# A two-layer decode kernel: one pool for all chunk places, half of wo ahead of time, V four chunks behind K, evenly paced chain pieces, fused end

## Chip, cores and metric

The kernel runs on one core of one Trainium2 chip. The time is device microseconds of one execution; most executions of one kernel agree within 0.3%. Times were taken on several chips, so kernels are compared by ratios: the mean time of one kernel's fast runs over the mean of the other's fast runs of the same rounds. This is not quite the ratio of the medians that are also quoted.

## The reference, cut to what matters

Eight rows (batch), one token each, run through attention, an MLP block, and the same attention and MLP a second time with the same caches and weights.

```python
x = x + A(layernorm(x), k_cache, v_cache, wq, wo)   # layer 1
x = x + B(layernorm(x), w1, w2, w3, w4)
x = x + A(layernorm(x), k_cache, v_cache, wq, wo)   # layer 2, same caches
x = x + B(layernorm(x), w1, w2, w3, w4)
# B=8, D=448, 16 query heads, 8 K/V heads, 4096 keys, head size 256, F=1792, bf16
```

With one token, both kernels leave out B's w1/w2 branch, whose shifted columns are all zero. K and V of a row are 32 chunks of 1 MB. Both layers need all of them, but layer 2 of a row can only begin when the row's layer 1 is through its *chain*: wo, norm, w3, GELU, w4, norm and the next query projection.

## The kernel before

Two K/V heads make a *pair*: four K chunks and four V chunks. Ten of a row's chunks are *kept* in SBUF from layer 1 until layer 2; everything else goes through a ring of five places. Loads leave in one fixed order through one queue, and each load has its place fixed in advance:

```python
        if key in kept:
            where[it] = NS + kept.index(key)      # one of ten bound places
            if ps == 0: loads.append(it)
        else:
            where[it] = r % NS                    # ring of NS = 5
            r += 1; loads.append(it)
...
    def emit_loads(most=None):
        while loads and not held[where[loads[0]]] and n != most:
            it = loads.pop(0)                     # strictly in order
```

A K chunk is transposed on VectorE, multiplied by q on TensorE (scores); exponentials run on ScalarE; a V chunk is multiplied by the probabilities (PV). The chain of a row is a generator. Its pieces are put between the chunks as fast as one or two a step:

```python
    hurry = (0, 1, Bn - 2, Bn - 1)
    def step(item=True):
        for kind in ("chain", "last"): ...
            for _ in range(2 if item and b in hurry and kind == "chain" else 1):
                if next(g, gens) is gens: ...
```

The end of the program is serial: the last row's wo, norm, w3, GELU, w4, and an output row in one partition (`...` is cut):

```python
    nc.vector.tensor_mul(var, mv[:, 0, :], mv[:, 0, :])
    nc.vector.tensor_sub(var, mv[:, 1, :], var)
    nc.vector.tensor_scalar_max(var, var, 0.0)
    nc.vector.tensor_scalar_add(ve[:, 0, :], var, EPS)
    nc.vector.reciprocal(ve[:, 1, :], ve[:, 0, :])   # second of two norms in a row
...
    for c in range(HC):                              # 14 matmuls of 448 columns
        nc.tensor.matmul(o_row[:], HT[:, c, :], w4_sb[:, c, :], ...)
```

The softmax here doesn't subtract the row's maximum and nothing guards it: scores larger than these inputs give would overflow.

## Time and profile before

| | before |
|---|---|
| time, median of 4 runs | 1195.3 us (1194.5 to 1197.7) |
| profiled span | 1196.4 us (of an execution of 1198.7 us, 3.4 above the median) |
| data moved | 465.91 MB |
| TensorE / VectorE busy | 55% / 47% |

From the page of the kernel before: the span, TensorE's busy tenths in 40 slices of 30 us, the granted TensorE clock, the DMA engines' busy tenths, the rate, and what the chain of waits that ended last is made of.

```profile
span 1196.4 us, 36650 instructions
...
PE   3133674357634774357634675357743674368765
...
PEclk9999997555655566555655557555665557555555
DMA  9999999999999999999999999999999999999792
GB/s 350 375 421 420 407 343 407 420 418 325 378 422 420 392 414 412 420 421 373 418 421 420 399 397 404 422 420 382 420 420 421 398 354 405 420 410 346 280 360 124
...
DMA 54%; PE 22%; DVE 17%; SPq 3%; issue 2%; POOL 1%; DVEq 0%; POOLq 0%; ACT 0%; ACTq 0%
```

The rate has a plateau at 420 to 422 GB/s and dips below it; loads are the largest part of the chain of waits. So the span can be read as a floor, 465.9 MB at 421 GB/s = 1107 us, plus lost DMA time. In the windows view (start and length of a stretch, busy time of PE, PE's weight loads, DVE, ACT and POOL with instruction counts, granted clock, DMA share, GB/s) the loss of a stretch is length × (1 − GB/s / 421).

```profile
48.00:140.00 92.00, 36.70 (x898) 26.78 (x902) 42.98 (x27) 7.01 (x14) 0.00 (x0) 1.00 1.01 420
140.00:190.00 50.00, 37.26 (x1034) 30.89 (x1030) 23.54 (x55) 5.04 (x10) 1.26 (x2) 0.95 0.93 359
...
264.00:316.00 52.00, 39.89 (x1041) 32.37 (x1039) 25.47 (x57) 7.01 (x14) 1.25 (x2) 0.54 0.91 340
...
944.00:1000.00 56.00, 39.59 (x1150) 32.10 (x1146) 27.45 (x53) 6.64 (x13) 1.25 (x2) 0.61 0.95 364
...
1070.00:1104.00 34.00, 27.07 (x698) 22.86 (x700) 16.66 (x54) 4.07 (x9) 1.25 (x2) 0.51 0.93 348
1104.00:1160.00 56.00, 39.14 (x1134) 35.68 (x1126) 26.96 (x49) 5.73 (x12) 2.59 (x1) 0.55 0.81 311
...
1177.20:1196.40 19.20, 10.37 (x152) 6.55 (x152) 4.78 (x29) 0.21 (x1) 0.70 (x1) 0.61 0.00 1
```

The first line is an undisturbed stretch. The next four are *chain stretches*: a row's chain runs between the chunks, chunks are freed late, and the queue waits. The 1104 line is the last row's stretch, the last line the tail without loads.

Short pieces of the timeline (start, length, engine, line, operation; in brackets the idle time before it and what ended it).

At the end of the program: the last PV, the sum onto x, the last matmuls, the cast of the output row.

```profile
1177.23 1.01 PE L587 MATMUL o_111<-ptw,slot_79 128*128 128x2 bf16 x32 [0.98 <-DMA slot_79<-in_A_v_cache_dram]
...
1180.13 0.16 DVE L709 TENSOR_TENSOR xT<-xT,o_112 128x4 f32<-128x4 f32 x1 [1.60 <-PE o_112 L309]
...
1189.76 3.93 PE L725 MATMUL o_row<-w_sb,HT_t 128*1 128x448 bf16 x14
...
1193.72 0.61 DVE L734 CAST slot_87<-o_row 1x448 bf16<-1x448 f32 x1 [5.78 <-PE o_row L725]
```

The last PV waits for the last load, and 18.2 us (1178.2 to 1196.4) follow it.

### The profile page before, as it was taken

What the parts mean: (1) busy time and instruction counts of PE and PEld (TensorE: products, weight loads), DVE (VectorE), ACT (ScalarE), POOL (GpSimd) and SP (SyncE); (2) the same over time, 40 slices, a digit from 0 to 9 for tenths busy, and PEclk for the clock granted to TensorE, in tenths of its full rate; (3) what the DMA queues carried; (4) which work ended last, traced back from release to release, by engine and by line L of the source; (5) the groups of instructions that cost most, each with busy time, mean ns of one, the idle gap of its engine ahead of it and who ended that gap; (6) DMA issues with size and microseconds to landing.
All of it is one profiled execution on the core that took longest, in us unless ns stands there. A gap on an engine that the chain in (4) does not pass through costs nothing.

```text
span 1196.4 us, 36650 instructions
## 1 busy us (share of the span) xinstructions
PE 660.9 (55%) x17225; PEld 521.2 (44%) x17225; DVE 565.3 (47%) x770; ACT 115.4 (10%) x233; POOL 15.6 (1%) x25
## 2 busy tenths in 40 slices
PE   3133674357634774357634675357743674368765
PEld 2122553245423563246522564235532553256654
DVE  5144454445444535456444554445354535444451
ACT  0000101001110111010101011101110111011100
POOL 0000000000000000000000000000000000000000
PEclk9999997555655566555655557555665557555555
DMA  9999999999999999999999999999999999999792
GB/s 350 375 421 420 407 343 407 420 418 325 378 422 420 392 414 412 420 421 373 418 421 420 399 397 404 422 420 382 420 420 421 398 354 405 420 410 346 280 360 124
DMA packets 69494, 465.91 MB, mean 389 GB/s; under 512 B 7120, under 2 KB 13152, under 8 KB 13664
## 3 DMA queue, kind: packets, MB, share of 16 engines
q1 hardware_dynamic: 69344, 463.58, 96.1%
q8 instruction: 134, 2.20, 0.7%
q14 instruction: 16, 0.13, 0.0%
HBM read 463.54 MB, written 0.01 MB: 387 GB/s over the span
## 4 chain that ended last, share of the span: by engine, by line
DMA 54%; PE 22%; DVE 17%; SPq 3%; issue 2%; POOL 1%; DVEq 0%; POOLq 0%; ACT 0%; ACTq 0%
DMA slot_78<-in_A_k_cache_dram 10%; DMA slot_80<-in_A_k_cache_dram 8%; DMA slot_81<-in_A_k_cache_dram 8%; DMA slot_87<-in_A_k_cache_dram 7%; DMA slot_79<-in_A_k_cache_dram 6%; DMA slot_82<-in_A_k_cache_dram 6%; DMA slot_83<-in_A_k_cache_dram 5%; PE y_ps L309 5%; PE sc_110 L532 4%; PE sc_109 L532 4%; DMA slot_92<-in_A_k_cache_dram 3%; DVE slot_78 L525 3%; DVE slot_81 L525 3%; DVE slot_80 L525 2%; DVE slot_79 L525 2%; DVE slot_82 L525 2%
## 5 line engine op out<-in xcount | busy, mean ns | idle before, releaser
L532 PEld LDWEIGHTS <-qbd 128*8 128x8 bf16 x8192 | 199.6, 112 | 496.7 <-issue 340.3
L573 PEld LDWEIGHTS <-ptw 128*8 128x8 bf16 x3840 | 115.8, 116 | 45.0 <-issue 16.3
L525 DVE STREAM_TRANSPOSE slot_78<-slot_78 128x2048 uint32<-128x2048 uint32 x34 | 78.5, 2310 | 87.6 <-DMA slot_78<-in_A_k_cache_dram 87.5
L525 DVE STREAM_TRANSPOSE slot_82<-slot_82 128x2048 uint32<-128x2048 uint32 x31 | 71.6, 2309 | 65.1 <-DMA slot_82<-in_A_k_cache_dram 64.9
L525 DVE STREAM_TRANSPOSE slot_79<-slot_79 128x2048 uint32<-128x2048 uint32 x32 | 73.9, 2308 | 59.4 <-DMA slot_79<-in_A_k_cache_dram 59.1
L525 DVE STREAM_TRANSPOSE slot_80<-slot_80 128x2048 uint32<-128x2048 uint32 x33 | 76.2, 2308 | 43.2 <-DMA slot_80<-in_A_k_cache_dram 42.9
L525 DVE STREAM_TRANSPOSE slot_81<-slot_81 128x2048 uint32<-128x2048 uint32 x30 | 69.2, 2308 | 44.7 <-DMA slot_81<-in_A_k_cache_dram 44.3
L541 ACT ACTIVATE p_n<-sc_110 128x512 bf16<-128x512 f32 x32 | 42.3, 1321 | 338.3 <-PE sc_110 L532 338.3
L541 ACT ACTIVATE p_n<-sc_109 128x512 bf16<-128x512 f32 x32 | 42.3, 1322 | 314.0 <-PE sc_109 L532 314.0
L309 PEld LDWEIGHTS <-wo_sb 128*128 128x128 bf16 (+1 forms) x1600 | 63.3, 125 | 16.4 <-issue 15.9
L309 PE MATMUL y_ps<-OT,wo_sb 128*128 128x1 bf16 (+1 forms) x1280 | 52.2, 176 | 6.6 <-DVE OT L424 5.7
L265 PEld LDWEIGHTS <-wq_sb 128*128 128x128 bf16 x1152 | 34.9, 105 | 27.3 <-issue 25.5
L532 PE MATMUL sc_110<-slot_78,qbd 128*8 128x128 bf16 x480 | 15.6, 304 | 48.0 <-DVE slot_78 L525 41.0
L561 ACT CAST ptw<-misc 128x128 bf16<-128x128 f32 x64 | 17.6, 275 | 252.8 <-PE misc L554 248.2
L532 PE MATMUL sc_109<-slot_78,qbd 128*8 128x128 bf16 x608 | 18.9, 296 | 36.4 <-DVE slot_78 L525 29.2
L265 PE MATMUL q_ps<-xb_126,wq_sb 128*128 128x1 bf16 x1024 | 32.0, 165 | 12.6 <-DVE xb_126 L253 10.2
L532 PE MATMUL sc_109<-slot_80,qbd 128*8 128x128 bf16 x576 | 18.1, 299 | 31.4 <-DVE slot_80 L525 26.8
L532 PE MATMUL sc_109<-slot_81,qbd 128*8 128x128 bf16 x512 | 16.0, 298 | 30.0 <-DVE slot_81 L525 25.2
L291 DVE TENSOR_SCALAR qbd<-misc,quad 128x64 bf16<-128x64 f32 x64 | 13.9, 278 | 39.5 <-PE misc L285 39.5
L532 PE MATMUL sc_110<-slot_82,qbd 128*8 128x128 bf16 x576 | 18.1, 299 | 26.0 <-DVE slot_82 L525 21.8
L532 PE MATMUL sc_109<-slot_79,qbd 128*8 128x128 bf16 x448 | 14.0, 297 | 31.6 <-DVE slot_79 L525 27.0
L532 PE MATMUL sc_110<-slot_79,qbd 128*8 128x128 bf16 x576 | 17.8, 296 | 24.6 <-DVE slot_79 L525 18.3
(193 smaller groups left out, 896.4 us busy)
## 6 DMA issues: line engine op xcount, KB each, us to landing
slot_81<-in_A_v_cache_dram SPq DMA_DIRECT2D x40, 1024.0 KB, 10.3
slot_79<-in_A_v_cache_dram SPq DMA_DIRECT2D x39, 1024.0 KB, 9.0
slot_82<-in_A_v_cache_dram SPq DMA_DIRECT2D x39, 1024.0 KB, 11.4
slot_78<-in_A_v_cache_dram SPq DMA_DIRECT2D x37, 1024.0 KB, 9.0
slot_80<-in_A_v_cache_dram SPq DMA_DIRECT2D x37, 1024.0 KB, 10.5
slot_78<-in_A_k_cache_dram SPq DMA_DIRECT2D x34, 1024.0 KB, 10.5
slot_80<-in_A_k_cache_dram SPq DMA_DIRECT2D x33, 1024.0 KB, 11.3
slot_79<-in_A_k_cache_dram SPq DMA_DIRECT2D x32, 1024.0 KB, 9.7
```

The costliest lines, as they stand in the source:

```text
L265: nc.tensor.matmul(q_ps[:, j * Hq + h, :], w, xbs(nb)[:, xi, :], start=(fc == 0), stop=(fc == 3),)
L291: nc.vector.tensor_scalar_mul(qbd[:, :, :, a, :], qs.rearrange("p e (f g u h) -> p (e f) u g h", f=2, u=2, h=2)[:, :, u], quad[:, a : a + 1],)
L309: nc.tensor.matmul(r, w[:, i, lo:hi], rhs(i), start=(first and fc == 0 and i == rows[0]), stop=(stop and i == rows[-1]), skip_group_check= ...
L525: nc.vector.transpose(w, w)
L532: nc.tensor.matmul(sc[32 * k : 32 * k + 8, 128 * x : 128 * x + 128], qbd[:, ep, gp].rearrange("p a h -> p (a h)"), kv[:, k, 2 * half + e2, ...
L541: nc.scalar.activation(p_sb[:].rearrange("p t i x -> p x t i"), sc[:].rearrange("p (x t i) -> p x t i", x=4, t=4), ACT.Exp, scale=scale_ex ...
L561: nc.scalar.copy(ptw[:, :, :, 6:8], pt_ps.rearrange("p t k (a h) -> p a (t k) h", a=4),)
L573: nc.tensor.matmul(o_ps[32 * q : 32 * q + 8, 256 * (g // 4) : 256 * (g // 4) + 256], ptw[:, a, 4 * (y % 4) + y // 4, w : w + 8], v[:, y * ...
```

## The change

Its intent: let any freed place take the next load; take work out of the chain's tight stretch and spread the rest evenly; shorten the serial end. The core of the diff, with cuts:

```diff
-            where[it] = r % NS
+    places = list(range(NC))                     # NC = 15, one pool
...
-        while loads and not held[where[loads[0]]] and n != most:
+        while loads and places and n != most:
+            p = where[it] = places.pop(0)
...
-        if j >= 5:                               # V five chunks behind K
+        if j >= LAG:                             # LAG = 4
...
+    def first_half(b, st):                       # heads 0-7 through wo, early
+        yield from half(st["o"], st["z"], 0, OT[:, :, :, 0])
+        yield from add_half(y_ps, OT, 0, 1, True, 2)
...
+            if e["n"] < e["of"] * (idx - e["at"] + 1) / max(e["until"] - e["at"], 1):
+                e["n"] += 1                      # as many pieces as the items passed
...
+            nc.vector.scalar_tensor_tensor(var, mv[:, 0], mv[:, 0], mv[:, 1],
+                ALU.mult, ALU.subtract, reverse1=True)
+        nc.vector.tensor_scalar(ve[:, 0], var, 0.0, EPS, ALU.max, ALU.add)
+            nc.vector.tensor_scalar(ve[:, 1], var, 0.0, EPS * EPS / (1 + EPS), ALU.max, ALU.add)
...
     for c in range(HC):
-        nc.tensor.matmul(o_row[:], HT[:, c, :], w4_sb[:, c, :], ...)
+        for q in range(4):                       # four column groups, 112 columns each
+            nc.tensor.matmul(o_row[32 * q : 32 * q + 1, :], HT[:, c, :],
+                             w4_sb[:, c, W * q : W * q + W], ...)
```

The last row's wo product is also taken in smaller pieces, so that 20 matmuls and not 40 follow the last PV.

## The prediction

> What bounds the kernel now. It streams its caches through one DMA queue: the page counts 465.9 MB. The windows view gives 420 to 421 GB/s in every undisturbed stretch (48 to 140, 316 to 400, 460 to 536, 1000 to 1070 us). The Trainium skill, "DMA: Bandwidth & Descriptors", section "Where 436 GB/s comes from", puts the ceiling of the 16 engines at 435 GB/s; this trace never sustains over about 424, so I use 421. 465.9 MB at 421 GB/s is 1107 us. The other 89 us of the 1196 us span are lost DMA time, by the same view (length x (1 - GB/s / 421)):
> - start, 0 to 48 us, 348 GB/s: 8 us.
> - eight stretches in which a row's chain (wo, MLP, next q) runs between the chunks: 7.4, 10.0, 3.3, 3.4, 4.3, 2.7, 7.6, 5.9 us, sum 45.
> - the end before the last landing, 1104 to 1177 us, 311 then 373 GB/s: 17 us.
> - after it: 19 us of pure tail.
> TensorE is busy only 55%, VectorE 47%; but in the chain stretches TensorE is busy about 75 to 80%, and the timeline shows K transposes every 5.7 us where two loads need 4.9: chunks are freed late and the queue waits.
>
> What the change does. Traffic, K transposes (2.31 us each), scores (1.02 us a chunk) and PV (about 1 us) stay.
> 1. One pool of 15 places: while the ten kept chunks are held both versions have five. It gains where kept places are empty: the start, and the last row, where places of ten resident chunks can take the last 22 loads, which now queue for five.
> 2. Half of wo moves into earlier, idle items: the order shows 80 wo matmuls and one output transposition fewer in the chain, 4 to 5 us of TensorE.
> 3. V lag 4: two items more for the chain. Pacing: the order shows row 1's chain spread over about 14 items, one piece an item, instead of two on many. P's transposition now stands right before its PV, so TensorE may wait about 0.5 us a pair for ScalarE's copy; not critical where DMA leads.
> 4. VectorE: fused operations, 704 to 641; about 0.2 us each.
> 5. Fused end, critical in full: last wo piece 40 to 20 matmuls (-0.8), norm and GELU about eight VectorE operations fewer (-1.7), x transposed before the hidden layer is ready rather than after (-1.7), 14 matmuls of 448 columns (3.9 us) become 56 of 112 on four column groups (about 1.7 us, estimated from 56 small matmuls in 1.63 us), output cast 0.61 to 0.2. Tail 19.2 to about 12.5 us.
>
> Sum (estimate): 1107 + start 8 + chain stretches 45 to about 14 + end 17 to about 4 + tail 12.5 = 1145 us. The chain's parts still alternate VectorE and TensorE between transposes, so I don't expect the stretches to vanish.
>
> Predicted 1145 us, 80% range 1128 to 1166. Faster by over 2%: 0.91; within 2%: 0.08; slower: 0.01.
>
> Right if: the page still moves 466 MB; chain stretches show 400 GB/s or more; the stretch before the last landing is near 420 GB/s; the tail is 12 to 13 us. Step 1 is wrong if DMA still drops near 300 GB/s in the last 90 us; step 3 if chain stretches stay near 340 to 360 GB/s.
>
> What would make it wrong: serial latency (transpose, scores, chain piece, transpose) rather than amount of work limits the stretches; consumers lag so far at the end that early loads only lengthen the tail; the P copy stalls PV.

## More of the kernel before

In a chain stretch, from the norm's sum to the first w3 matmul:

```profile
271.36 0.56 PE L201 MATMUL st<-xs_t,one 128*128 128x2 f32 x2
...
275.00 0.14 DVE L253 CAST xb_126<-xn_t 64x1 bf16<-64x1 f32 x1
275.15 1.63 PE L327 MATMUL h_ps<-xb_126,w_sb 128*128 128x1 bf16 x56 [2.28 <-DVE xb_126 L253]
```

TensorE stands idle for 2.28 us until VectorE's string of small operations is done. Over the whole kernel its waits for the norm's result (tile xb) sum to 33.2 us.

## The result and the profile after

The changed kernel takes 1151.64 us (median of 4 runs, 1150.7 to 1154.7) against 1195.3; the ratio is 0.9636 (95% interval 0.9613 to 0.9659). From its page:

```profile
span 1149.6 us, 36516 instructions
...
PE   3134677557645665456754576536765476547786
...
DMA  9999999999999999999999999999999999999993
GB/s 353 375 421 420 419 398 414 420 421 396 418 421 420 420 419 419 420 402 413 419 419 420 405 417 419 420 420 399 419 420 420 410 399 414 420 419 393 412 420 143
...
PE 5%; DVE 1%; issue 1%; DMA 1%; POOL 0%; ACT 0%; POOLq 0%; DVEq 0%; ACTq 0%
```

The dips are nearly filled. (The chain of waits could be followed back only through the last 90 us here; its shares are of the whole span and say nothing about the rest.) The same windows view, for stretches of the changed kernel:

```profile
148.00:192.00 44.00, 34.09 (x948) 26.71 (x940) 23.47 (x40) 5.15 (x11) 0.68 (x2) 0.99 1.00 402
264.00:312.00 48.00, 34.23 (x1012) 27.01 (x1015) 23.35 (x38) 7.09 (x15) 0.55 (x1) 0.64 1.01 406
...
908.00:960.00 52.00, 37.54 (x977) 29.96 (x969) 24.89 (x50) 5.24 (x11) 1.25 (x2) 0.51 1.00 399
1044.00:1070.00 26.00, 19.84 (x522) 16.45 (x521) 14.85 (x28) 2.77 (x6) 0.89 (x2) 0.50 0.98 383
1070.00:1130.00 60.00, 46.41 (x1242) 38.19 (x1226) 29.19 (x52) 7.80 (x17) 2.59 (x1) 0.59 1.01 417
1130.00:1149.60 19.60, 12.79 (x350) 11.62 (x350) 3.89 (x25) 0.49 (x2) 0.70 (x1) 0.50 0.05 20
```

With the loss formula, where the time went (us; "predicted" is the sum in the prediction):

| term | before | predicted | after |
|---|---|---|---|
| data at 421 GB/s | 1107 | 1107 | 1107 |
| start, 0 to 48 us | 8 | 8 | 7.8 |
| chain stretches | 45 | 14 | 13.6 (1.4 to 2.7 in each of seven) |
| last row's stretch, to the last landing | 17 | 4 | 0.6 |
| last microseconds without loads | 19 | 12.5 | 18.7 |
| other small dips | 1 | 0 | 2 |

The norm's place in a chain stretch is shorter: VectorE needs fewer operations between the sum and the first w3 matmul, and TensorE idles 0.91 us instead of 2.28. Its waits for xb sum to 8.6 us, where they were 33.2.

```profile
1042.21 0.59 PE L212 MATMUL st<-t,one 128*128 128x2 f32 x2
...
1044.38 0.59 DVE L249 TENSOR_SCALAR xb_126<-t 128x3 bf16<-128x3 f32 x3 [0.81 <-POOL t L232]
...
1044.66 1.02 PE L336 MATMUL h_ps<-xb_126,w_sb 128*128 128x1 bf16 x32 [0.91 <-DVE xb_126 L249]
```

The end, with the same four marks as before (last PV, sum onto x, last matmuls, cast):

```profile
1136.83 0.99 PE L608 MATMUL o_111<-ptw,slot_82 128*128 128x2 bf16 x32
...
1138.95 0.16 DVE L756 TENSOR_TENSOR xT<-xT,o_112 128x4 f32<-128x4 f32 x1 [0.86 <-PE o_112 L318]
...
1145.22 1.48 PE L778 MATMUL o_row<-w_sb,HT_t 128*1 128x112 bf16 x56 [0.35 <-DVE HT_t L359]
1146.75 0.27 DVE L787 CAST slot_87<-o_row 128x112 bf16<-128x112 f32 x1 [1.58 <-PE o_row L778]
```

After the last PV 11.8 us follow instead of 18.2: the fused end saves 6.4 us. But the last PV no longer waits for a load. Loads are over by about 1132 us, 5 us before it starts. The chain of waits shows why (pieces in order of time: start, length, what; "issue" is time in which the engine waited for nothing that the profile shows):

```profile
1069.19 8.24 DMA slot_79<-in_A_v_cache_dram
...
1078.20 2.01 issue
...
1087.62 1.80 PE y_ps L318 x64
...
1090.81 2.17 issue
...
1136.02 1.81 PE o_111 L608 x64
```

After 1077 us no load stands in it. With 15 places the loads run ahead, and TensorE, with scores, PV and the wo and MLP matmuls of seven rows, ends last. It is busy 46.4 of the 60 us to 1130. Of the other 13.6 us, 7.3 are five gaps inside groups of weight loads (at 1078, 1086, 1091, 1110 and 1116 us), before which TensorE waits for no semaphore; the two "issue" pieces are among them, and the last section returns to them. So the lag at the end is not the amount of work alone.

### The profile page after: what moved, and what is told of

Read it like the earlier page. It is cut to its first block, busy times and chain, and to the rows that moved or that the text cites. A ratio compares the mean times of both kernels' runs of the same rounds, so it can differ in the third digit from the quotient of the medians.

```text
span 1149.6 us, 36516 instructions
## 1 busy us (share of the span) xinstructions
PE 677.8 (59%) x17177; PEld 522.2 (45%) x17177; DVE 554.0 (48%) x712; ACT 114.1 (10%) x234; POOL 15.6 (1%) x25
## 5 line engine op out<-in xcount | busy, mean ns | idle before, releaser
L594 PEld LDWEIGHTS <-ptw 128*8 128x8 bf16 x3968 | 110.2, 111 | 78.0 <-issue 29.4
L546 DVE STREAM_TRANSPOSE slot_79<-slot_79 128x2048 uint32<-128x2048 uint32 x19 | 43.8, 2308 | 39.0 <-DMA slot_79<-in_A_k_cache_dram 36.0
L546 DVE STREAM_TRANSPOSE slot_86<-slot_86 128x2048 uint32<-128x2048 uint32 x19 | 43.9, 2311 | 38.6 <-DMA slot_86<-in_A_k_cache_dram 36.0
L546 DVE STREAM_TRANSPOSE slot_81<-slot_81 128x2048 uint32<-128x2048 uint32 x18 | 41.6, 2309 | 37.4 <-DMA slot_81<-in_A_k_cache_dram 37.4
L318 PE MATMUL y_ps<-OT,wo_sb 128*128 128x1 bf16 (+1 forms) x1280 | 55.1, 176 | 3.0 <-issue 3.0
L546 DVE STREAM_TRANSPOSE slot_89<-slot_89 128x2048 uint32<-128x2048 uint32 x16 | 37.0, 2310 | 32.1 <-DMA slot_89<-in_A_k_cache_dram 32.0
L546 DVE STREAM_TRANSPOSE slot_88<-slot_88 128x2048 uint32<-128x2048 uint32 x15 | 34.6, 2308 | 29.8 <-DMA slot_88<-in_A_k_cache_dram 29.8
L546 DVE STREAM_TRANSPOSE slot_90<-slot_90 128x2048 uint32<-128x2048 uint32 x14 | 32.3, 2308 | 31.9 <-DMA slot_90<-in_A_k_cache_dram 31.9
L546 DVE STREAM_TRANSPOSE slot_82<-slot_82 128x2048 uint32<-128x2048 uint32 x14 | 32.3, 2307 | 29.5 <-DMA slot_82<-in_A_k_cache_dram 29.5
L546 DVE STREAM_TRANSPOSE slot_80<-slot_80 128x2048 uint32<-128x2048 uint32 x14 | 32.3, 2304 | 29.3 <-DMA slot_80<-in_A_k_cache_dram 29.3
L546 DVE STREAM_TRANSPOSE slot_84<-slot_84 128x2048 uint32<-128x2048 uint32 x12 | 27.7, 2309 | 37.5 <-DMA slot_84<-in_A_k_cache_dram 37.3
L546 DVE STREAM_TRANSPOSE slot_78<-slot_78 128x2048 uint32<-128x2048 uint32 x13 | 30.0, 2310 | 29.4 <-DMA slot_78<-in_A_k_cache_dram 29.4
L274 PEld LDWEIGHTS <-wq_sb 128*128 128x128 bf16 x1152 | 33.9, 104 | 18.2 <-issue 16.6
L546 DVE STREAM_TRANSPOSE slot_83<-slot_83 128x2048 uint32<-128x2048 uint32 x13 | 30.0, 2306 | 25.2 <-DMA slot_83<-in_A_k_cache_dram 25.2
L546 DVE STREAM_TRANSPOSE slot_92<-slot_92 128x2048 uint32<-128x2048 uint32 x12 | 27.6, 2304 | 21.8 <-DMA slot_92<-in_A_k_cache_dram 21.8
L546 DVE STREAM_TRANSPOSE slot_87<-slot_87 128x2048 uint32<-128x2048 uint32 x10 | 23.1, 2311 | 20.6 <-DMA slot_87<-in_A_k_cache_dram 20.5
## 6 DMA issues: line engine op xcount, KB each, us to landing
slot_82<-in_A_v_cache_dram SPq DMA_DIRECT2D x17, 1024.0 KB, 17.6
slot_88<-in_A_v_cache_dram SPq DMA_DIRECT2D x17, 1024.0 KB, 13.6
```

Source lines behind the costliest of these rows:

```text
L274: nc.tensor.matmul(q_ps[:, j * Hq + h, :], w, xbs(nb)[:, xi, :], start=(fc == 0), stop=(fc == 3),)
L318: nc.tensor.matmul(r, w[:, i, lo:hi], rhs(i), start=(first and fc == 0 and i == rows[0]), stop=(stop and i == rows[-1]), skip_group_check= ...
L546: nc.vector.transpose(w, w)
L594: nc.tensor.matmul(o_ps[32 * q : 32 * q + 8, 256 * (g // 4) : 256 * (g // 4) + 256], ptw[:, a, 4 * (y % 4) + y // 4, w : w + 8], v[:, y * ...
```

## The experiments

The question is which part earned the 43.7 us. Theory A (mine): lighter, evenly spread chains cured the stretches, and the pool counts only at the end. Rival B: the pool did most. Effects are given as (ratio − 0.9636) × 1195.3 us. Each ratio has an interval of about ± 0.0023, so a difference of two is known to about ± 4 us: effects of 2 to 4 us are not settled by times alone.

| kernel | median us | ratio to before | effect against the changed kernel |
|---|---|---|---|
| fixed_places | 1162.24 | 0.9735 | +11.8 |
| old_steps | 1159.58 | 0.9705 | +8.2 |
| late_wo | 1153.52 | 0.9655 | +2.3 |
| early_wo7 | 1148.03 | 0.9609 | −3.2 |
| lag5 | 1155.56 | 0.9666 | +3.6 |
| old_output | 1154.37 | 0.9657 | +2.5 |
| old_vector_ops | 1162.22 | 0.9717 | +9.7 |
| fixed_and_old_steps | 1169.35 | 0.9776 | +16.7 |
| ahead | 1154.46 | 0.9655 | +2.3 |
| ahead_wo7 | 1154.66 | 0.9644 | +1.0 |
| ahead_old_vector | 1163.03 | 0.9725 | +10.6 |
| before_pool | 1186.98 | 0.9923 | (−9.2 against before) |

All gave correct results. The first four, the next four and the last four each shared a chip.

### fixed_places: the pool undone

```diff
-        while loads and places and n != most:
-            p = where[it] = places.pop(0)
+        while loads and not held[home[loads[0]]] and n != most:
+            p = where[it] = home[it]     # five ring places, ten bound ones
```

> The changed kernel with only the pool undone: five ring places and ten places bound to the kept chunks, as before. Theory A (the chain stretches were cured by lighter and evenly spread chains; the pool helps only where kept places are empty, at the end): chain stretches stay near 400 GB/s, the windows between the last row's first chunk and the last landing fall back to about 310 to 350 GB/s, time about 1161 us (the last row took 78 us before and 68 us after, so +10). Rival B (the pool did most of it, because any freed place can take the next load): chain stretches fall back to 340 to 380 GB/s and the time is 1172 us or more.

The time came out as A said, but A's reason only in part. The last row's stretch did fall back: 378 GB/s from 1066 to 1143 us. But row 0's chain stretch got worse too, which A had excluded. Its windows:

```profile
176.00:180.00 4.00, 4.00 (x99) 3.10 (x100) 0.38 (x2) 0.00 (x0) 0.00 (x0) 1.00 0.94 356
180.00:184.00 4.00, 2.47 (x88) 1.99 (x88) 2.94 (x3) 1.59 (x3) 0.00 (x0) 1.00 0.19 68
184.00:188.00 4.00, 3.96 (x154) 3.34 (x155) 1.77 (x1) 0.00 (x0) 0.00 (x0) 1.00 0.89 301
```

The changed kernel in the middle one:

```profile
180.00:184.00 4.00, 4.00 (x92) 3.20 (x88) 2.88 (x3) 1.34 (x2) 0.00 (x0) 1.00 1.01 420
```

The load queue of fixed_places, in the timeline:

```profile
175.88 7.92 SPq L547 DMA_DIRECT2D slot<-in_A_k_cache_dram  x2
183.84 1.68 SPq L547 DMA_DIRECT2D slot<-in_A_v_cache_dram  x1
```

Two K loads span 7.9 us. In the order of the queue the second is the next row's kept chunk of the third pair, bound to a place whose old chunk had not had its turn; other places, freed just before, stood empty (this follows from the order of the program, not from the trace). In the same time the changed kernel issued seven loads more. So the pool also earns where row 0's kept places turn over: a queue in strict order stops at its first blocked load. The order has such a block at every row's turnover, but only row 0's shows as lost time: from 140 to 200 us the rate is 371 GB/s against the changed kernel's 406, which is 5.0 us, while from 200 to 1040 us both run at 415. Most of the rest of the 8.7 us between the two spans (1158.3 and 1149.6) is lost at the end.

### old_steps: the pacing undone

```diff
-            if e["n"] < e["of"] * (idx - e["at"] + 1) / max(e["until"] - e["at"], 1):
+            for _ in range(2 if item and e["b"] in hurry and kind == "chain" else 1):
```

> The changed kernel with only the pacing undone: pieces of the chain are taken as fast as before (two a K chunk in hurried rows, one otherwise, one more after each V chunk). Theory A: chain stretches fall back to 350 to 380 GB/s, time 1160 to 1172 us. Rival B: stretches stay near 400 GB/s, time under 1156 us.

The time lies just under A's range and above B's. The stretches of three hurried rows fell to 353 GB/s (140 to 166 us), 373 (918 to 954) and 336 (1044 to 1072, where the changed kernel has 386), but row 1's stayed at 401. The last of them:

```profile
1044.00:1072.00 28.00, 21.40 (x524) 16.96 (x524) 15.53 (x34) 2.08 (x5) 1.25 (x2) 0.50 0.94 336
```

Pacing is worth about 8 us, mostly at those rows.

### late_wo: the early 80 matmuls back in the chain

```diff
     def first_half(b, st):
         yield from half(st["o"], st["z"], 0, OT[:, :, :, 0])
-        yield from add_half(y_ps, OT, 0, 1, True, 2)
     def chain(b, st):
         yield from half(st["o"], st["z"], 1, OT[:, :, :, 0])
+        yield from add_half(y_ps, OT, 0, 1, True, 2)
```

> The changed kernel with only the first half's 80 wo matmuls moved back into the chain (its output transposition stays early; the chain's pieces are 33 instead of 30, spread over the same items). Theory A (the amount of TensorE work in the stretch counts): 80 matmuls at 29 to 58 ns are 2.3 to 4.6 us a row, eight rows, partly taken up by the five prefetched chunks: time 1156 to 1166 us. Rival (only the number of alternations counts): within 2 us of the changed kernel's 1151.6.

A missed: 1153.5 us, an effect not clear of zero; the rival's "within 2 us" holds, barely. When spread evenly, 80 more matmuls in a row's stretch cost little: about 2 us over all rows, known to ± 4 us. (A first form that moved the output transposition too deadlocked when built and was not run.)

### early_wo7: a further step

```diff
+        if b == Bn - 2:                       # in first_last, after row 6's kept pairs
+            y7 = ps_m.tile([128, 4, nb], FP32, tag="last")
+            yield from add_half(y7, OT2[:, :, :, :nb], 1, nb, True, 1)
...
-        yield from out_cols(lambda i: OT2[:, i % 2, i // 2, :nb], wo_sb, NB2, 0, nb, 1)
+        yield from add_half(st["y7"], OT2[:, :, :, :nb], 0, nb, False, 2)
```

> A further step: the wo product of the first seven rows in the second layer is halved too; the 80 matmuls for heads 8 to 15 run right after row 6's kept pairs, so only 80 stay in the last row's stretch. Theory A's reading of the end (from about 1077 us on the chain of waits holds no load, TensorE is what ends last): 80 matmuls of 58 ns are 4.6 us less, time 1147 to 1149 us, the last landing stays where it is and the gap between it and the end shrinks. Rival (the end is set by loads or by serial latency): within 1 us of 1151.6.

The time came out as expected. The loads still end at about 1132 us, and less follows them; its windows:

```profile
1130.00:1132.00 2.00, 1.74 (x50) 1.64 (x49) 0.23 (x2) 0.00 (x0) 0.00 (x0) 0.50 0.42 169
1132.00:1146.50 14.50, 7.68 (x225) 6.57 (x222) 3.47 (x22) 0.21 (x1) 0.70 (x1) 0.50 0.01 5
```

In the changed kernel 17.6 us follow 1132. That the 80 matmuls earned this is not shown, though. The gaps inside groups of weight loads sum to 3.1 us (two gaps) in the last 90 us here and to 7.3 us in the changed kernel; that difference alone is as large as the gain. In the chain of waits loads stand again, until 1120 us. And ahead_wo7 below, with the same edit, does not repeat the gain. At 1148.0 us this is the fastest kernel tried; its five runs (1147.5 to 1148.3) lie under all four of the changed kernel, though not in the same rounds, and the intervals of the two ratios overlap (0.9586 to 0.9631 against 0.9613 to 0.9659).

### lag5: V five chunks behind K again

```diff
-    LAG = 4
+    LAG = 5
-            if c == 0 and n > 0:
+            if c == 1 and n > 0:              # P's transposition one K chunk later
```

> The changed kernel with V five chunks behind K, as before (P's transposition after the second K chunk of the next pair). Theory: the chain loses two of its items, so its pieces are packed a little tighter, against about 0.4 us a pair that TensorE no longer waits for ScalarE's copy: time 1152 to 1157 us. Rival (the copy's wait costs where TensorE is the limit): 1147 to 1151 us.

Within the expectation. The last chain stretch shows it: 370 GB/s from 1050 to 1086 us. The wait for ScalarE's copy that lag 4 brings is real (in the changed kernel PV's weight loads waited 35 times for it, 18.0 us in all, at most 0.5 us each). That it costs less than the two lost items fits the time, but +3.6 is within the error.

### old_output: the last output row undone

```diff
-    o_row = ps_m.tile([128, W], FP32, tag="chain")
+    o_row = ps_m.tile([1, D], FP32, tag=bank[0])      # x transposed after the hidden layer
-        for q in range(4): nc.tensor.matmul(o_row[32 * q : 32 * q + 1, :], ...)   # 112 columns
+        nc.tensor.matmul(o_row[:], HT[:, c, :], w4_sb[:, c, :], ...)              # 448 columns
```

> The changed kernel with only the last output row undone: x transposed after the hidden layer, 14 matmuls of 448 columns into one partition, a 448 wide cast. From the hidden layer's last VectorE operation to the end of the cast it was 6.4 us before and 1.9 us after, and all of it is serial: time 1151.6 + 4.5 = 1156 us (1155 to 1157).

Less than expected: +2.5 by the ratio, 3.0 between the two profiled spans (1152.6 and 1149.6). My 6.4 us for "before" was not all the old output's: here GELU's last operation to the end of the cast takes 5.8 us (1144.8 to 1150.6), because x's transposition starts before GELU ends. The gain there is 5.8 − 1.9 = 3.9 us, and the four-partition output gives some back: from the cast's end to the program's end it takes 2.6 us, the single row 2.0.

### old_vector_ops: norm and GELU operations undone

```diff
-            nc.vector.scalar_tensor_tensor(var, mv[:, 0], mv[:, 0], mv[:, 1], ...)
+        nc.vector.tensor_mul(var, mv[:, 0, :], mv[:, 0, :])
+        nc.vector.tensor_sub(var, mv[:, 1, :], var)
+        nc.vector.tensor_scalar_max(var, var, 0.0)      # and so on, as in the kernel before
```

> The changed kernel with only the VectorE operations of the norm and of GELU undone. At the serial end about eight more operations of 0.2 us each, 1.6 us; in the chain stretches they are mostly taken up: time 1153 to 1156 us. Rival (VectorE's serial latency limits the stretches): 1158 us or more.

My expectation failed: 1162 us. Its windows of two hurried rows:

```profile
918.00:962.00 44.00, 31.16 (x771) 24.75 (x772) 23.18 (x55) 3.98 (x9) 1.25 (x2) 0.50 0.99 376
1040.00:1080.00 40.00, 29.70 (x720) 23.82 (x712) 23.15 (x57) 3.43 (x7) 1.25 (x2) 0.50 0.95 364
```

Over its seven chain stretches the loss sums to 22.7 us against 13.6; 3 us more are in the tail. In the timeline the idle time before w3 is back, and in all TensorE waits 21.1 us for xb, against 8.6 in the changed kernel:

```profile
1053.31 0.99 PE L333 MATMUL h_ps<-xb,w_sb 128*128 128x1 bf16 x32 [2.28 <-DVE xb L259]
```

About ten operations of 0.16 us are nothing against VectorE's 565 us, but TensorE takes its work here in the order of the program: in the 2.28 us for which it waits, it runs no scores and no PV, so no place comes free. The Trainium skill, "VectorE: DVE Perf Modes", section "The TRN2 errata", says that operations from SBUF pay a fixed cost per instruction. The traces agree: 128x1 takes 0.16 us and 128x28 0.19 us, so it is the count of operations that matters.

### fixed_and_old_steps: pool and pacing both undone

> Pool and pacing undone together. If the two gains add up: 1151.6 + 10.6 + 8.0 = 1170 us. If each hides the other's gain because the same few prefetched chunks take up what is left when only one is missing: 1174 us or more. If they overlap: under 1166 us.

The edit is that of the two kernels together. 1169 us: this fits two gains that add up, 11.8 + 8.2 against 16.7, within the error; an overlap of a few microseconds is not excluded.

### ahead, ahead_wo7, ahead_old_vector: the K transposition one item earlier

Theory C, made after old_vector_ops: the pair is a serial loop, and the K transposition (2.3 us) can be taken off it.

```diff
         else:                                  # a V item
             st = state[ps, b]
+            transpose_ahead(idx + 1)           # the next item's K chunk
```

> The changed kernel with each K chunk's transposition put on VectorE one item earlier, at the start of the V item ahead of it. Theory C (after undoing the VectorE operations cost 10.6 us): in a chain stretch one pair is a serial loop through two engines, K transposition 2.3 us, scores 1 us, chain pieces, VectorE pieces, next transposition; taking the 2.3 us off that loop removes most of the 13 us still lost in the stretches: time 1141 to 1147 us, stretches above 410 GB/s. Rival A (amount of TensorE work in the stretch): within 2 us of 1151.6.

> The same, with the wo product of the seven rows halved as in early_wo7, which gained 3.6 us at the end. The two act at different places and should add: 1138 to 1143 us.

> The early transposition with the VectorE operations of norm and GELU as before. Theory C: with the transposition off the loop the longer norm is taken up in the stretches and only the serial end pays (its tail was 2.5 us longer): 2 to 5 us above the kernel 'ahead'. Rival (each VectorE operation costs wherever it stands): 9 us or more above 'ahead'.

C's remedy failed: "ahead" is not faster (+2.3, within the error; near rival A's number, though A's reason had already failed in late_wo). The timeline shows that the wait only moved:

```profile
1049.06 1.02 PE L336 MATMUL h_ps<-xb,w_sb 128*128 128x1 bf16 x32 [2.46 <-DVE xb L249]
...
1063.96 1.87 PE L274 MATMUL q_ps<-xb,wq_sb 128*128 128x1 bf16 x64 [2.88 <-DVE xb L249]
```

Now the transposition stands ahead of the norm's operations on VectorE, and TensorE waits for the norm instead: 22.3 us in all for xb, against 8.6 in the changed kernel. ahead_old_vector is 8.6 us above ahead on the same chip, close to the rival's 9: the operations cost their time wherever the transposition stands. ahead_wo7 missed too. The 3 us of early_wo7 did not reappear clearly beside ahead (ratio 0.9644 against 0.9655); why is left open.

### before_pool: the pool alone, in the kernel before

```diff
-        while loads and not held[where[loads[0]]] and n != most:
+        while loads and places and n != most:
+            p = where[it] = places.pop(0)      # and two freed places as scratch at the end
```

> The kernel before with the pool alone. Undoing the pool cost the changed kernel 10.6 us; the kernel before loses 17 us before its last landing and about 5 us where row 0's kept places turn over, and keeps its longer chains: 10 to 15 us faster than before, 1180 to 1185 us. If the pool pays only together with the other parts: within 5 us of before.

9.2 us faster by the ratio, a little under the expectation. Its stretch from 1096 to 1158 us runs at 400 GB/s, but 27 us without loads follow (19 in the kernel before). The loads came early and the consumer was not ready: the same exchange as in the changed kernel. Row 0's stretch (140 to 190 us) hardly gained, 368 GB/s against 359; row 1's (264 to 316) did, 373 against 340. So the turnover's 5 us, on which the expectation counted, did not come back here; why is not shown.

## Why the prediction was right, and where not

The measured 1151.6 us lies in the range; the mean estimate was 6.6 us low. About 1.8 us of this is no step of the argument: the sum was built from a profiled span, and a run's time is that much longer than its span (1151.35 against 1149.6). Of the prediction's own tests, the traffic (466 MB) and the stretch before the last landing (417 GB/s) held; of the seven chain stretches six have 399 to 406 GB/s and the last 383; the tail missed.

- **Floor, start, chain stretches.** 1107, 8 and 14 us were predicted and measured. This sum is what held the prediction. But the prediction does not work out how 45 becomes 14, and two of the parts that it names were sized wrongly (below); that the term fits so closely is in part luck.
- **The mis-sized term: "Tail 19.2 to about 12.5 us".** The fused end itself was sized well: 6.4 us saved after the last PV, 6.8 predicted. What was missing is the consumer's lag: the last PV started 5 us after the last landing, so 18.7 us were still lost there. The prediction named this ("consumers lag so far at the end that early loads only lengthen the tail") but gave it no microseconds. The term before it erred the other way (4 predicted, 0.6 measured), so half of the miss is cancelled. It is the same exchange: a pool that is never short moves the end from the loads to TensorE. early_wo7 fits the view that TensorE's work is then worth taking away, but does not show it.
- **"It gains where kept places are empty: the start, and the last row"** was incomplete. fixed_places showed the turnover of row 0's kept places as well, a queue stopped for 7 us at one bound place. Undoing the pool costs 11.8 us in all.
- **"Half of wo moves into earlier, idle items ... 4 to 5 us of TensorE"** led to the right total through a wrong reason. late_wo: about 2 us over all rows, not clear of zero.
- **"VectorE: fused operations ... about 0.2 us each"** was counted only at the end (1.7 us). Undoing them cost 9.7 us, mostly in the chain stretches. The warning "serial latency ... rather than amount of work" was the right one.
- **Lag and copy.** The 0.5 us wait a pair was there and did not show in the time, as predicted.

One part at a time, the undone parts sum to 11.8 + 8.2 + 9.7 + 3.6 + 2.5 + 2.3 = 38 of 43.5 us (43.5 is the gain by the ratio, 43.7 by the medians). The rest (smaller wo pieces at the end, the order of halves, overlaps) was not separated. lag5, old_output and late_wo are, by times alone, within the error.

## What to carry to other kernels

When loads bind, split the span into data at the plateau rate plus lost DMA time by stretch, and ask of each stretch what holds back the freeing of places. In a stretch where an engine does two jobs in the order of the program, a handful of 0.16 us operations on another engine that it must wait for can cost more than 80 matmuls that it need not wait for (here 9.7 us against about 2). A deeper pool removes waits in the queue, but at the end it hands the limit to the next engine, so look at that engine's last work in the same step.

## What the Trainium skill lacked or had wrong

- "Runtime: NRT & Kernel Launch", section "Instruction fetch mechanics", says the cost of crossing a 16 KiB instruction block is mostly hidden. In the changed kernel TensorE has 19 gaps over 0.5 us between weight loads of one and the same group, with no wait for a semaphore before them, 25.8 us in all (counted from the trace itself, not from a view); every one of them ends 1.2 to 1.7 us after the end of an instruction packet (134 packets of this queue, 2.20 MB, are on the page). "Mostly" holds, since the other packets have no such gap beside them, but what is left is not small: the two "issue" pieces of about 2 us shown above are among the 19. This is a coincidence in time, not tested by a run.
- "TensorE: Matmul & The Clock Gate", Part 1, says activity releases the throttle. In the kernel before, the granted clock was 1.00 from 48 to 140 us with TensorE busy 37 of 92 us, and 0.54 from 264 to 316 us with it busy 40 of 52 us. No run here shows why.
- "DMA: Bandwidth & Descriptors", "Where 436 GB/s comes from", says that for transfers between HBM and SBUF the HBM side, about 358 GB/s, binds. This single core, which reads its caches from HBM, held 420 to 421 GB/s in every undisturbed stretch, for loads of 1 MB issued from one queue; that is nearer to the 435 GB/s that the same section gives for the ports.
- No page that I read has the effect of fixed_places: where the program issues its loads in strict order through one queue, all 16 DMA engines are left nearly idle when the first load's place is taken (68 GB/s for 4 us while other places were free).
